# Interleaving two expert layers at their seam, spreading operand splits over two steps, and writing outputs out one block at a time

## Chip, core and metric

The kernel runs on one core of one Trainium2 chip. The metric is the device time of one execution in microseconds (us), as the median of several runs. Five engines work side by side, each through its own queue in the order in which the program emits instructions: TensorE (PE, matrix products, with weight loads shown apart as PEld), VectorE (DVE), ScalarE (ACT), GpSimd (POOL) and SyncE (SP, which here only issues DMAs).

## The reference, cut to what matters

```python
x = rmsnorm_attention(q, k, v, g_norm)            # linear attention, (2304, 512)
h = x @ w_in; x = (h * sigmoid(h)) @ w_out        # first experts: 512 -> 2048 -> 512
p = domain_probs / (domain_probs.sum(-1, keepdims=True) + 1e-9)
out = zeros(2304, 512)
for e in range(4):                                # second experts: 512 -> 1024 -> 512 each
    h = maximum(x @ w1[e], 0)
    out += p[:, e:e+1] * (h @ w2[e])
```

Everything is float32. Each operand is split into a high part and a rest, and a product is the sum of three PE products (high by high, high by rest, rest by high).

## The kernel before

The first part is one hand-written order (`PROGRAM`, and then the loop at L750) of attention and the first experts. The 2048 hidden features are 16 chunks, taken as 4 groups of 4, and the 2304 tokens are five tiles. A unit is one chunk of one tile: `mm1` (12 matmuls into a bank of the PSUM pool `ps_h`, evacuated by ACT and DVE in `ev1` and `ev2`), and two units later (`LAG`) `mm2` (12 matmuls into the four banks of `ps_a`). After the fourth chunk of a tile, `flush` adds the four banks to the SBUF array `acc` on DVE, and the next tile's `mm2` must wait for the banks to be free. `divide` (L709) normalizes the probabilities on DVE, turns them with one PE transpose and sends them to DRAM; it is emitted between an `mm1` and an `mm2`.

The second part is the class `Second`. It has 24 steps: `NP` = 3 token blocks t of 768 tokens, by `E2` = 8 half experts q; n = 8t + q. A step does a 2 by 2 block product in seven products instead of eight (a Strassen-Winograd form): `first(n, k)`, k = 0 to 6, 12 matmuls each, which accumulate into two PSUM tiles x and z of the pool `ps1`. Its weight operands are the sums `sum1` (s1 to s4) split by `op1`, its feature operands the sums `sumx` (t1 to t4) split by `opx`. A split is two instructions: ACT copies the high part (L139), and DVE or POOL subtracts it (L140). Then `keep` (ACT) and `add` (DVE) take the sums out of PSUM, `hid` (ACT, then DVE) makes the hidden blocks, `second(n, b, d)` is 12 matmuls each for four blocks b and two halves d into `ps2` (two tiles of two banks), `weigh` multiplies by the probabilities on DVE, and for q > 0 POOL adds the result to `acc` (L261).

`events` gives each of these a time in slots; a slot is one group of 12 matmuls, and a step is 15 slots. All events are sorted by slot and emitted, so the slots are the order in every queue. `first(n, k)` stands at slot 1 + 2k of step n and the eight `second` of step n at the even places of step n + 1, so the two alternate on PE. Weight operands of step n are made in step n - 1 (`before` is its first slot). For a new token block (q = 0) `opx(t, k)` stands at `before + 2k + 2.5`, so all seven feature operands and four sums are made within step n - 1. The events of step 0 with a slot below zero (`early`) are dealt out over the last eight units of the first experts. After a block's last step `leave` turns the output with PE transposes: two groups of 128 tokens share one tile of `ps2`, each with 4 transposes (L269), an ACT copy (L271) and a DMA issued by ACT (L272).

Of the kernel before, what the change touches and what calls it, by code (L numbers as in the profile page):

```python
# [8 lines left out]
F32 = mybir.dt.float32  # L9
# [4 lines left out]
AF = mybir.ActivationFunctionType  # L14
# [66 lines left out]
class Second:  # L81
# [14 lines left out]
    SLOTS = 15  # L96

    BLOCKS = ((0, 1), (0, 0), (1, 1), (1, 0))

    def __init__(self, tc, w, acc, p_dram, ident, out):  # L100
        self.tc, self.nc = tc, tc.nc
# [9 lines left out]
    def open_right(self):  # L111
# [4 lines left out]
        self.s_p = self.open(st, "s", 3, side="right")  # L116
        self.raw1_p = self.open(st, "raw1", 5, side="right")

    def open_left(self):
        st = ExitStack()  # L120
        self.stacks.append(st)
        self.w2_p = self.open(st, "w2", 5)
        self.raw2_p = self.open(st, "raw2", 4)
        self.h_p = self.open(st, "hid", 6)
        self.f_p = self.open(st, "f", 4)
        self.m_p = self.open(st, "m", 2)
        self.pb_p = self.open(st, "pb", 2)
        self.o_p = self.open(st, "o2", 2)
        self.ps1 = self.open(st, "ps1", 2, space=PSUM)
        self.ps2 = self.open(st, "ps2", 2, space=PSUM)  # L130

    def close(self):
# [63 lines left out]
        self.nc.vector.tensor_tensor(f, b[a], b[c], op=ALU.subtract)  # L196
        self.t[t, name] = f

    def opx(self, t, k):
        name = self.B[k]  # L200
        src = self.t[t, name] if name[0] == "t" else self.sums(t, int(name[1]) - 1, int(name[2]) - 1)
        x = self.x_p.tile([128, 2, 2, HN], F32R, tag=f"x{k}", name="x2")
        self.split(x, src)
        self.x[t, k] = x


# [24 lines left out]
    def hid(self, n, i, j, name):  # L231
# [4 lines left out]
        self.nc.vector.scalar_tensor_tensor(h[:, 1], src, 0.0, h[:, 0].bitcast(F32), op0=ALU.max, op1=ALU.subtract)  # L236
        self.h[n, i, j] = h

    def second(self, n, b, d):
        i, j = self.BLOCKS[b]  # L240
        if d == 0:
            self.ps[n, b] = self.ps2.tile([128, 2, 512], F32, tag="ps2", name="ps_o")
        o = self.ps[n, b][:, d, :HN]
# [9 lines left out]
    def weigh(self, n, b):  # L253
        t, q = divmod(n, E2)
        i, j = self.BLOCKS[b]
        p = self.pb[t, q // 2][:, j * HN : j * HN + HN].unsqueeze(1).to_broadcast([128, 2, HN])
        a = self.sums(t, i, j)
        m = a if q == 0 else self.m_p.tile([128, 2, HN], F32, tag="m", name="m")
        self.nc.vector.tensor_tensor(m, self.ps[n, b][:, :, :HN], p, op=ALU.mult)  # L259
        if q:  # L260
            self.nc.gpsimd.tensor_tensor(a, a, m, op=ALU.add)  # L261

    def leave(self, t, b):

        p = self.ps2.tile([128, 2, 512], F32, tag="ps2", name="ps_t")
        for k in range(2):
            c = (b + k) * 128
            for d in range(KC):
                self.nc.tensor.transpose(p[:, k, d * 128 : d * 128 + 128], self.acc[:, t, d, c : c + 128], self.ident)  # L269
            o = self.o_p.tile([128, DM], F32, tag="o2", name="o2")  # L270
            self.nc.scalar.activation(o, p[:, k, :], AF.Copy)  # L271
            self.nc.scalar.dma_start(out=self.out[t * PW + c : t * PW + c + 128, :], in_=o)  # L272


    def events(self):

        ev = []

        def put(slot, f, *a):
            ev.append((slot, len(ev), f, a))  # L280

        pool = self.nc.gpsimd
        for n in range(self.steps):
            t, q = divmod(n, E2)
# [48 lines left out]
            if q % 2 == 0:  # L333
                put(after - 8, self.load_p, t, q // 2)
            for b in range(4):
                for d in range(2):
                    put(after + 4 * b + 2 * d, self.second, n, b, d)
                put(after + 4 * b + 3.2, self.weigh, n, b)
                put(after + 4 * b + 3.21, self.ps.pop, (n, b))
            for i in range(2):  # L340
                for j in range(2):
                    put(after + (10.1, 14.1)[1 - j], self.h.pop, (n, i, j))
                    put(after + (6.1, 14.1)[i], self.w2.pop, (n, i, j))
            if q % 2 == 1:
                put(after + 15.3, self.pb.pop, (t, q // 2))
            if q == E2 - 1:
                for b in range(0, PW // 128, 2):
# [7 lines left out]
    def run(self):  # L355
        for s, _, f, a in self.events():
            if s >= 0:
                f(*a)


# [1 line left out]
def attention_moe_kernel(ctx: ExitStack, tc: tile.TileContext, kv, qt, g2, probs, wd, w, out):  # L362
    nc = tc.nc


    left, right, psum = ExitStack(), ExitStack(), ExitStack()
# [11 lines left out]
    ring_p = on(left, "ring", RING)  # L378
    h_p = on(left, "h", 3)
    tmp_p = on(left, "tmp", 6)  # L380
    ps_h = on(psum, "ps_h", 4, space=PSUM)
    ps_a = on(psum, "ps_a", 1, space=PSUM)

    ident = const.tile([128, 128], F32, name="ident")
# [302 lines left out]
    with tc.manual_schedule():  # L687
# [21 lines left out]
        def divide():  # L709
# [2 lines left out]
            nc.vector.reciprocal(prs, prs)  # L712
            nb = NT // 128
            nc.vector.tensor_tensor(prn, pr.rearrange("p b e -> p e b"), prs.rearrange("p b o -> p o b").to_broadcast([128, 4, nb]), op=ALU.mult)
            p = ps_h.tile([4 * nb, 128], F32, tag="p", name="p_p")
            nc.tensor.transpose(p, prn.rearrange("p e b -> p (e b)"), ident)
            t = tmp_p.tile([4 * nb, 128], F32, tag="tmp", name="p_t")
# [45 lines left out]
        moe.run()  # L763
        moe.close()


# [32 lines left out]
```

## Time and profile before

| | us |
|---|---|
| median of 3 runs (1280.91 to 1282.31) | 1281.31 |
| the profiled execution | 1280.92 |
| its span, first to last instruction | 1278.8 |
| PE busy in the span | 1225.7 (96%) |
| DVE busy | 743.5 (58%) |
| ACT busy | 497.2 (39%) |
| POOL busy | 490.2 (38%) |
| mean granted TensorE clock | 0.984 of full speed |

The span is cut into stretches below by the times at which PE's groups start. Attention ends at about 165 us, the first experts at 484.8 us, and the 24 steps of the second experts run to 1264 us; what remains is the end of the outputs. In a stretch where PE is the limit, PE's busy time is the stretch itself and its granted clock is 1.00; stretches with a smaller busy time or a lower clock are where time can be won.

### The profile page before, as it was taken

Reading aid. Unit: us, or ns where it says so; the run is one execution under the profiler, and the core shown is the slowest. Engines: PE = TensorE matmul, PEld = TensorE weight load, DVE = VectorE, ACT = ScalarE, POOL = GpSimd, SP = SyncE. Lnnn points to the kernel's source line nnn. Section 1 sums busy time; section 2 is a strip of 40 time slices with the busy share of each in tenths; the row PEclk is TensorE's granted clock in tenths of the full one; section 3 lists DMA queues with packets and bytes.
Section 4 is the critical chain, followed back from the end, with each engine's and each line's share of the span. In section 5 each row is a group of like instructions: output and inputs, shape, how many; then the busy total and the mean of one; then the engine's idle time right before and its main releaser. Section 6 shows DMA issues by size and latency. Waiting matters only on the chain.

```text
span 1278.8 us, 17258 instructions
## 1 busy us (share of the span) xinstructions
PE 1225.7 (96%) x6705; PEld 1149.1 (90%) x6705; DVE 743.5 (58%) x978; ACT 497.2 (39%) x811; POOL 490.2 (38%) x338
## 2 busy tenths in 40 slices
PE   6889999999999988999999899999998999999997
PEld 6778798887888878999999899999998999999996
DVE  4985546554654475565566865555558655665531
ACT  4555443333332244333334434333334443333321
POOL 2563423302300002255555452455554424555543
PEclk9999999998999999999999999999999999999998
DMA  9523111002200013222222133222221223222201
GB/s 329 187 70 108 33 51 51 16 1 100 74 1 1 1 39 107 77 69 79 67 78 67 50 96 100 78 67 82 72 84 47 85 79 85 73 85 68 62 9 49
DMA packets 72981, 91.90 MB, mean 72 GB/s; under 512 B 8956, under 2 KB 62788, under 8 KB 72900
## 3 DMA queue, kind: packets, MB, share of 16 engines
q1 hardware_dynamic: 70020, 86.05, 21.9%
q10 hardware_dynamic: 2880, 4.76, 1.0%
q8 instruction: 52, 0.85, 0.3%
q14 instruction: 29, 0.24, 0.1%
HBM read 86.02 MB, written 4.76 MB: 71 GB/s over the span
## 4 chain that ended last, share of the span: by engine, by line
PE 79%; DVE 5%; ACT 2%; issue 1%; POOLq 0%; POOL 0%; ACTq 0%; DVEq 0%
PE ps_o L250 29%; PE ps_x L217 14%; PE a L656 12%; PE p_h L618 11%; PE ps_z L217 11%; DVE s L176 1%; PE ps_t L269 1%; DVE x L140 1%; DVE t L196 1%; DVE f L229 1%; DVE w L140 1%; ACT o L271 1%; ACT w L139 0%; DVE hid L236 0%; ACT hid L235 0%
## 5 line engine op out<-in xcount | busy, mean ns | idle before, releaser
L250 PE MATMUL ps_o<-hid,w 128*128 128x384 f32 x2304 | 432.4, 337 | 9.4 <-ACT hid L235 7.4
L250 PEld LDWEIGHTS ps_o<-hid,w 128*128 128x128 f32 x2304 | 406.2, 189 | 11.4 <-ACT hid L235 8.3
L140 POOL TENSOR_TENSOR w<-raw,w 128x512 fp32r<-128x512 f32 x144 | 204.0, 1435 | 291.0 <-ACT w L139 169.8
L261 POOL TENSOR_TENSOR acc<-acc,m 128x768 f32<-128x768 f32 x84 | 162.9, 1940 | 254.0 <-DVE m L259 253.9
L217 PE MATMUL ps_x<-x,w 128*128 128x384 f32 x1152 | 217.4, 336 | 1.4 <-DVE f L229 1.4
L217 PEld LDWEIGHTS ps_x<-x,w 128*128 128x128 f32 x1152 | 202.4, 189 | 1.9 <-DVE f L229 1.8
L217 PE MATMUL ps_z<-x,w 128*128 128x384 f32 x864 | 161.8, 335 | 0.0
L217 PEld LDWEIGHTS ps_z<-x,w 128*128 128x128 f32 x864 | 151.0, 188 | 0.2 <-ACT f L224 0.2
L140 DVE TENSOR_TENSOR w<-s,w 128x512 fp32r<-128x512 f32 x96 | 95.1, 992 | 85.0 <-ACT w L139 85.0
L139 ACT ACTIVATE w<-raw 128x512 fp32r<-128x512 f32 x168 | 100.4, 624 | 63.8 <-issue 62.5
L656 PE MATMUL a<-h_hi,w_hi 128*128 128x512 f32 (+1 forms) x320 | 119.9, 375 | 3.5 <-DVE acc L668 3.5
L618 PE MATMUL p_h<-x_hi,w_hi 128*128 128x512 f32 (+1 forms) x320 | 120.3, 376 | 1.0 <-ACT o L554 1.0
L656 PE MATMUL a<-h_lo,w_hi 128*128 128x512 f32 (+1 forms) x320 | 119.3, 373 | 1.1 <-DVE h_lo L642 1.1
L618 PE MATMUL p_h<-x_lo,w_hi 128*128 128x512 f32 (+1 forms) x320 | 119.6, 374 | 0.4 <-DVE x_lo L604 0.4
L618 PE MATMUL p_h<-x_hi,w_lo 128*128 128x512 f32 (+1 forms) x320 | 119.7, 374 | 0.0
L656 PE MATMUL a<-h_hi,w_lo 128*128 128x512 f32 (+1 forms) x320 | 118.9, 372 | 0.0
L633 DVE TENSOR_TENSOR sg<-p_h,sg 128x512 f32<-128x512 f32 (+1 forms) x80 | 50.8, 637 | 102.5 <-ACT sg L632 102.2
L478 POOL TENSOR_TENSOR cv_a<-wd_raw,cv_a 128x512 f32<-128x512 f32 x28 | 37.5, 1340 | 188.8 <-DVE cv_a L476 79.1
L139 ACT ACTIVATE w<-s 128x512 fp32r<-128x512 f32 x96 | 60.2, 628 | 113.8 <-DVE s L176 111.3
L632 ACT ACTIVATE sg<-p_h 128x512 f32<-128x512 f32 (+1 forms) x80 | 44.4, 556 | 150.3 <-PE p_h L618 145.4
L224 ACT ACTIVATE f<-ps_x 128x768 f32<-128x768 f32 x48 | 39.1, 814 | 156.7 <-PE ps_x L217 156.7
L259 DVE TENSOR_TENSOR m<-ps_o,pb 128x768 f32<-128x768 f32 x84 | 80.3, 956 | 29.8 <-PE ps_o L250 27.8
(112 smaller groups left out, 1414.6 us busy)
## 6 DMA issues: line engine op xcount, KB each, us to landing
raw<-in_w SPq DMA_DIRECT2D x384, 128.0 KB, 2.4
wd_raw<-in_wd SPq DMA_DIRECT2D x28, 512.0 KB, 3.8
pb<-p_dram SPq DMA_DIRECT2D x12, 384.0 KB, 4.2
out<-o ACTq DMA_DIRECT2D x18, 256.0 KB, 2.0
kv_first_lo<-in_kv SPq DMA_DIRECT2D x6, 512.0 KB, 9.7
q_raw<-in_qt SPq DMA_DIRECT2D x6, 512.0 KB, 8.1
kv_first_hi<-in_kv SPq DMA_DIRECT2D x5, 512.0 KB, 11.1
acc<-in_wd SPq DMA_DIRECT2D x4, 512.0 KB, 10.9
```

The source lines that it names most:

```text
L139: self.nc.scalar.activation(t[:, 0], f, AF.Copy)
L140: (eng or self.nc.vector).tensor_tensor(t[:, 1], f, t[:, 0].bitcast(F32), op=ALU.subtract)
L217: self.nc.tensor.matmul(p[:, f, :HN], w[:, a, cols], x[:, b, kp, :], start=self.FRESH[k] and kp == m == 0, stop=kp == 1 and m == 2, skip_g ...
L224: self.nc.scalar.activation(t, self.ps[n, c][:, :, :HN], AF.Copy)
L250: self.nc.tensor.matmul(o, w[:, u, cols], h[:, v, kp, :], start=m == 0, stop=m == 11)
L259: self.nc.vector.tensor_tensor(m, self.ps[n, b][:, :, :HN], p, op=ALU.mult)
L261: self.nc.gpsimd.tensor_tensor(a, a, m, op=ALU.add)
L478: nc.gpsimd.tensor_tensor(a, l, a, op=ALU.mult)
L618: nc.tensor.matmul(p[:, :n], wt[:, 0, cols], xt[:, kc, :], start=k == 0, stop=k == 3 * KC - 1)
L632: nc.scalar.activation(sg[:, :n], p[:, :n], AF.Sigmoid)
L633: nc.vector.tensor_tensor(sg[:, :n], p[:, :n], sg[:, :n], op=ALU.mult)
L656: nc.tensor.matmul(o, a, m, start=first and k == 0, stop=last and k == 2)
```

## The change

Five things change.

1. At the seam of the two parts: the PSUM pool of `mm1` is closed before the last two `mm2`, `ps1` is opened in its place, and `first(0, 0)` and `first(0, 1)` are emitted ahead of the last `mm2` but one and the last `mm2`.
2. Feature operands: for t > 0 `opx(t, k)` stands at `before + 3.4k + 4`, so it runs from slot 4 of step n - 1 to slot 9.4 of step n. For t = 0 the subtraction of k = 1, 3, 5 goes to POOL, and for step 0 all seven weight operands' subtractions do (before: two).
3. `leave` takes one group of 128 tokens for a PSUM tile, two calls after each of the first three blocks of the step after next.
4. The last step: blocks in another order (`LAST`), the sum to `acc` on DVE, the last block's two halves in PSUM tiles of their own and weighed apart, and `leave_last`, which turns pieces of the output as soon as they are final (6, 6, 6, 3 and 3 transposes), with DMAs issued by SP.
5. The transpose of the probabilities (`turn_p`) is emitted four units after `divide`.

```diff
+    LAST = ((0, 1), (1, 1), (0, 0), (1, 0))
...
+    def open_first(self):
+        st = ExitStack()
+        self.stacks.append(st)
+        self.ps1 = self.open(st, "ps1", 2, space=PSUM, side="right")
...
-    def opx(self, t, k):
+    def opx(self, t, k, eng=None):
...
-        self.split(x, src)
+        self.split(x, src, eng)
...
+    def end(self, n, b):
+        return n == self.steps - 1 and b == 3
...
-        if d == 0:
-            self.ps[n, b] = self.ps2.tile([128, 2, 512], F32, tag="ps2", name="ps_o")
+        if d == 0 or self.end(n, b):
+            self.ps[n, b, d] = self.ps2.tile([128, 2, 512], F32, tag="ps2", name="ps_o")
...
+            eng = self.nc.vector if n == self.steps - 1 else self.nc.gpsimd
+            eng.tensor_tensor(a, a, m, op=ALU.add)
...
+    def leave(self, t, k):
         p = self.ps2.tile([128, 2, 512], F32, tag="ps2", name="ps_t")
-        for k in range(2):
-            c = (b + k) * 128
-            for d in range(KC):
-                self.nc.tensor.transpose(p[:, k, d * 128 : d * 128 + 128], self.acc[:, t, d, c : c + 128], self.ident)
...
+        c = k * 128
+        for d in range(KC):
+            self.nc.tensor.transpose(p[:, 0, d * 128 : d * 128 + 128], self.acc[:, t, d, c : c + 128], self.ident)
...
+    def leave_last(self, j, ds):
+        t, nk, m = NP - 1, HN // 128, 128 * len(ds)
+        p = self.ps1.tile([128, 2, 512], F32, tag="ps1", name="ps_t").rearrange("p a b -> p (a b)")[:, : nk * m]
+        for k in range(nk):
+            for i, d in enumerate(ds):
+                c, r = j * HN + k * 128, k * m + i * 128
+                self.nc.tensor.transpose(p[:, r : r + 128], self.acc[:, t, d, c : c + 128], self.ident)
+        o = self.f_p.tile([128, 2, HN], F32, tag="f", name="o").rearrange("p a b -> p (a b)")[:, : nk * m]
+        self.nc.scalar.activation(o, p, AF.Copy)
...
+        self.nc.sync.dma_start(out=to, in_=o.rearrange("p (k c) -> p k c", k=nk))
...
-                put(before + 2 * k + 2.3, self.op1, n, k, pool if k in (1, 6) else None)
+                put(before + 2 * k + 2.3, self.op1, n, k, pool if k in (1, 6) or n == 0 else None)
...
-                at = [before + 2 * k + 2.5 for k in range(7)]
+                at = [before + 3.4 * k + 4 for k in range(7)]
...
-                    put(at[k], self.opx, t, k)
+                    put(at[k], self.opx, t, k, pool if t == 0 and k % 2 else None)
...
+                    if last and b == 3:
+                        put(after + 4 * b + 2 * d + 1.2, self.weigh, n, b, d, 1)
...
+            if last:
+                for slot, j, ds in ((6.5, 1, (0, 1)), (10.5, 1, (2, 3)), (12.5, 0, (0, 1)), (15, 0, (2,)), (16, 0, (3,))):
+                    put(after + slot, self.leave_last, j, ds)
...
-                    put(after + 20 + 2 * b, self.leave, t, b)
+                        put(after + self.SLOTS + 4 * (k // 2) + 3.3, self.leave, t, k)
...
+            if s >= 0 and not (f == self.first and a[0] == 0 and a[1] < k):
...
+        put(at[2, 0, 0] + 4, 0, turn_p)
...
-        for u in units[-LAG:]:
+        psum_h.close()
+        moe.open_first()
+        for k, u in enumerate(units[-LAG:]):
+            moe.first(0, k)
             mm2(*u)
```

## Rows read from the trace of the kernel before

**Rows 1.** The page's first part: busy time, share of the span, and instructions by engine.
```profile
PE 1225.7 (96%) x6705; PEld 1149.1 (90%) x6705; DVE 743.5 (58%) x978; ACT 497.2 (39%) x811; POOL 490.2 (38%) x338
```

**Rows 2.** Waits of PE over the span: total us, how many, the longest.
```profile
PE ps_o L250 <- ACT hid L235: 7.4, 3, 2.8
...
PE p_p L716 <- DVE prn L714: 3.8, 1, 3.8
PE a L656 <- DVE acc L668: 3.5, 1, 3.5
```

**Rows 3.** Stretches: length, busy us of each engine, granted clock, DMA share, GB/s.
```profile
286.00:296.63 10.63, 6.87 (x26) 6.01 (x26) 2.24 (x6) 1.50 (x3) 0.00 (x0) 0.68 0.44 152
466.00:473.94 7.94, 4.47 (x14) 3.49 (x14) 6.44 (x11) 2.35 (x6) 0.00 (x0) 0.79 0.12 33
484.82:507.58 22.76, 19.03 (x97) 17.77 (x96) 14.48 (x18) 11.72 (x18) 8.09 (x6) 0.93 0.28 82
659.80:691.10 31.30, 31.30 (x183) 31.30 (x182) 18.74 (x20) 11.86 (x19) 16.17 (x10) 1.00 0.26 81
697.10:728.40 31.30, 27.74 (x159) 27.16 (x157) 26.66 (x27) 15.19 (x22) 12.90 (x7) 1.00 0.14 41
722.14:734.17 12.03, 8.36 (x37) 7.78 (x37) 10.92 (x12) 5.56 (x8) 4.93 (x3) 0.86 0.30 88
983.32:996.25 12.93, 9.49 (x37) 8.78 (x37) 10.92 (x12) 5.55 (x8) 5.84 (x4) 0.74 0.27 81
771.67:775.54 3.87, 3.18 (x22) 2.95 (x20) 2.28 (x3) 1.20 (x2) 0.17 (x1) 1.00 0.28 107
```

**Rows 4.** Chain that ended last: start, us, engine, line and matmuls of a group.
```profile
452.52 2.73 PE p_h L618 x12
...
518.16 2.08 PE ps_o L250 x12
```

**Rows 5.** Timeline, end of the first experts: start, us, engine, instruction, idle before, releaser.
```profile
468.76 2.48 DVE L668 TENSOR_TENSOR acc<-a,acc 128x512 f32<-128x512 f32 x4
```

**Rows 6.** Timeline of an undisturbed step (start 661.7 us): DVE, POOL, PE.
```profile
673.13 0.68 DVE L176 TENSOR_TENSOR s<-raw,raw 128x512 f32<-128x512 f32 x1
...
679.41 4.71 POOL L140 TENSOR_TENSOR w<-raw,w 128x512 fp32r<-128x512 f32 x3
...
681.19 1.77 DVE L176 TENSOR_TENSOR s<-raw,raw 128x512 f32<-128x512 f32 x1
682.88 0.94 DVE L229 TENSOR_TENSOR f<-ps_x,f 128x768 f32<-128x768 f32 x1
...
689.35 0.95 DVE L236 SCALAR_TENSOR_TENSOR hid<-f,hid 128x768 fp32r<-128x768 f32 x1
...
690.90 4.33 PE L250 MATMUL ps_o<-hid,w 128*128 128x384 f32 x24
```

**Rows 7.** Timeline at the seam: the last flush, the next DVE instruction, the first second product.
```profile
482.98 2.74 DVE L668 TENSOR_TENSOR acc<-a,acc 128x512 f32<-128x512 f32 x4 [3.41 <-PE a L656]
488.49 0.69 DVE L140 TENSOR_TENSOR w<-raw,w 128x512 fp32r<-128x512 f32 x1 [2.78 <-ACT w L139]
...
503.39 0.56 PE L250 MATMUL ps_o<-hid,w 128*128 128x384 f32 x1 [1.84 <-ACT hid L235]
```

**Rows 8.** Timeline of the first pair of output groups of the first token block.
```profile
771.67 0.60 PE L269 MATMUL ps_t<-ident,acc 128*128 128x128 f32 x4
...
772.95 0.66 PE L269 MATMUL ps_t<-ident,acc 128*128 128x128 f32 x4 [0.69 <-ACT o L271]
```

**Rows 9.** Timeline of the end, from the last block's weighing to the last DMA issue.
```profile
1264.43 0.96 DVE L259 TENSOR_TENSOR m<-ps_o,pb 128x768 f32<-128x768 f32 x1 [3.21 <-PE ps_o L250]
1265.47 1.80 POOL L261 TENSOR_TENSOR acc<-acc,m 128x768 f32<-128x768 f32 x1 [2.34 <-DVE m L259]
...
1267.33 0.44 PE L269 MATMUL ps_t<-ident,acc 128*128 128x128 f32 x2 [2.78 <-POOL acc L261]
...
1275.97 0.34 ACTq L272 DMA_DIRECT2D out<-o  x1
```

More of the change, by code (lines that the diff above doesn't have):

```diff
@@ L128, in open_left @@
         self.o_p = self.open(st, "o2", 2)
-        self.ps1 = self.open(st, "ps1", 2, space=PSUM)
         self.ps2 = self.open(st, "ps2", 2, space=PSUM)
@@ L237, in hid, with blocks @@
         self.h[n, i, j] = h
+    def blocks(self, n):
+        return self.LAST if n == self.steps - 1 else self.BLOCKS
+    def end(self, n, b):
+        return n == self.steps - 1 and b == 3
     def second(self, n, b, d):
-        i, j = self.BLOCKS[b]
-        if d == 0:
-            self.ps[n, b] = self.ps2.tile([128, 2, 512], F32, tag="ps2", name="ps_o")
-        o = self.ps[n, b][:, d, :HN]
+        i, j = self.blocks(n)[b]
+        if d == 0 or self.end(n, b):
+            self.ps[n, b, d] = self.ps2.tile([128, 2, 512], F32, tag="ps2", name="ps_o")
+        o = self.ps[n, b, d if self.end(n, b) else 0][:, d, :HN]
         m = 0
@@ L251, in second, with weigh @@
                     m += 1
-    def weigh(self, n, b):
+    def weigh(self, n, b, d=0, c=2):
         t, q = divmod(n, E2)
[L255 to L259, printed above, removed]
+        i, j = self.blocks(n)[b]
+        p = self.pb[t, q // 2][:, j * HN : j * HN + HN].unsqueeze(1).to_broadcast([128, c, HN])
+        a = self.sums(t, i, j)[:, d : d + c]
+        m = a if q == 0 else self.m_p.tile([128, 2, HN], F32, tag="m", name="m")[:, :c]
+        self.nc.vector.tensor_tensor(m, self.ps.pop((n, b, d))[:, d : d + c, :HN], p, op=ALU.mult)
@@ L260, in weigh @@
         if q:
-            self.nc.gpsimd.tensor_tensor(a, a, m, op=ALU.add)
-    def leave(self, t, b):
+            eng = self.nc.vector if n == self.steps - 1 else self.nc.gpsimd
+            eng.tensor_tensor(a, a, m, op=ALU.add)
+    def leave(self, t, k):
         p = self.ps2.tile([128, 2, 512], F32, tag="ps2", name="ps_t")
-        for k in range(2):
-            c = (b + k) * 128
-            for d in range(KC):
-                self.nc.tensor.transpose(p[:, k, d * 128 : d * 128 + 128], self.acc[:, t, d, c : c + 128], self.ident)
-            o = self.o_p.tile([128, DM], F32, tag="o2", name="o2")
-            self.nc.scalar.activation(o, p[:, k, :], AF.Copy)
-            self.nc.scalar.dma_start(out=self.out[t * PW + c : t * PW + c + 128, :], in_=o)
+        c = k * 128
+        for d in range(KC):
+            self.nc.tensor.transpose(p[:, 0, d * 128 : d * 128 + 128], self.acc[:, t, d, c : c + 128], self.ident)
+        o = self.o_p.tile([128, DM], F32, tag="o2", name="o2")
+        self.nc.scalar.activation(o, p[:, 0, :], AF.Copy)
+        self.nc.scalar.dma_start(out=self.out[t * PW + c : t * PW + c + 128, :], in_=o)
@@ new lines, in leave_last @@
+    def leave_last(self, j, ds):
[7 more added lines that the diff above has]
+        self.nc.scalar.activation(o, p, AF.Copy)
+        r = t * PW + j * HN
+        to = self.out[r : r + HN, ds[0] * 128 : ds[0] * 128 + m].rearrange("(k p) c -> p k c", p=128)
+        self.nc.sync.dma_start(out=to, in_=o.rearrange("p (k c) -> p k c", k=nk))
@@ L334, in events @@
                 put(after - 8, self.load_p, t, q // 2)
+            last = n == self.steps - 1
             for b in range(4):
@@ L337, in events @@
                     put(after + 4 * b + 2 * d, self.second, n, b, d)
[L338 to L347, printed above, removed]
-                    put(after + 20 + 2 * b, self.leave, t, b)
+                    if last and b == 3:
+                        put(after + 4 * b + 2 * d + 1.2, self.weigh, n, b, d, 1)
+                if not last or b < 3:
+                    put(after + 4 * b + 3.2, self.weigh, n, b)
+            if last:
+                for slot, j, ds in ((6.5, 1, (0, 1)), (10.5, 1, (2, 3)), (12.5, 0, (0, 1)), (15, 0, (2,)), (16, 0, (3,))):
+                    put(after + slot, self.leave_last, j, ds)
+            else:
+                for i in range(2):
+                    for j in range(2):
+                        put(after + (10.1, 14.1)[1 - j], self.h.pop, (n, i, j))
+                        put(after + (6.1, 14.1)[i], self.w2.pop, (n, i, j))
+                if q % 2 == 1:
+                    put(after + 15.3, self.pb.pop, (t, q // 2))
+                if q == E2 - 1:
+                    for k in range(PW // 128):
+                        put(after + self.SLOTS + 4 * (k // 2) + 3.3, self.leave, t, k)
         return sorted(ev, key=lambda e: e[:2])
@@ L353, in early, with run @@
         return [lambda f=f, a=a: f(*a) for s, _, f, a in self.events() if s < 0 and f != self.load2]
-    def run(self):
+    def run(self, k):
         for s, _, f, a in self.events():
-            if s >= 0:
+            if s >= 0 and not (f == self.first and a[0] == 0 and a[1] < k):
                 f(*a)
@@ L363, in attention_moe_kernel @@
     nc = tc.nc
-    left, right, psum = ExitStack(), ExitStack(), ExitStack()
+    left, right, psum, psum_h = (ExitStack() for _ in range(4))
     const = ctx.enter_context(tc.tile_pool(name="const", bufs=1))
@@ L380, in attention_moe_kernel @@
     tmp_p = on(left, "tmp", 6)
-    ps_h = on(psum, "ps_h", 4, space=PSUM)
+    ps_h = on(psum_h, "ps_h", 4, space=PSUM, side="right")
     ps_a = on(psum, "ps_a", 1, space=PSUM)
@@ L714, in divide, with turn_p @@
             nc.vector.tensor_tensor(prn, pr.rearrange("p b e -> p e b"), prs.rearrange("p b o -> p o b").to_broadcast([128, 4, nb]), op=ALU.mult)
+        def turn_p():
+            nb = NT // 128
             p = ps_h.tile([4 * nb, 128], F32, tag="p", name="p_p")
@@ L762, in attention_moe_kernel @@
         moe.open_left()
-        moe.run()
+        moe.run(LAG)
         moe.close()
```

## Prediction

> **What bounds the kernel now.** The page's first part comes first: PE is busy 96% of the span [rows 1], so time is won only where PE pauses, where it runs at a lower clock, or in the end that has no products. The list of PE's waits names who ends the pauses, and that they are few and long: 3.8 us at the probabilities, 3.5 us for a `flush`, 7.4 us in three waits for `hid` [rows 2]. The table of stretches then shows what each place costs, clock included [rows 3]. The scale is the group of 12 matmuls: 2.72 us at 512 columns and 2.08 us at 384 when undisturbed [rows 4]. An undisturbed step has PE busy for all of 31.30 us at clock 1.00, with DVE busy 18.74 us. The step in which a new token block's operands are made has DVE busy 26.66 us of 31.30 [rows 3]; there the in-order DVE queue makes `hid` late.
>
> Losses, as length less groups at full rate [rows 3, 4]. Probabilities: 10.63 less 12 matmuls of 256 columns (half of 2.72, about 1.4), 12 of 512 (2.72) and a transpose (0.1): 6.4 us, of which 3.76 is idle (10.63 - 6.87) and the rest is the clock of 0.68 behind it. Flush: 7.94 - 2.72 = 5.2 us. Seam: 22.76 us for eight groups (16.7): 6.1 us. The two block changes: three groups (6.25) each in 12.03 and 12.93: 5.8 and 6.7, together 12.5 us. Outputs of blocks 0 and 1: a pair adds 3.87 - 2.08 = 1.8 us, six pairs. End: from 1264.0 (last group's end) to 1278.8, 14.8 us.
>
> **The change part by part.** *Probabilities (change 5).* The wait goes: four units later, some 20 us, DVE has long finished. What stays is one transpose, 0.1 us, in the stream, and the DMA to DRAM on SP moves behind some weight loads, long before the step that needs it. Gain 6.3 us. If something else were late there, the idle 3.76 would return; the other units of that loop show no such pause, so I allow 5 to 6.4.
>
> *Earlier splits to POOL (change 2, t = 0).* The flush starts at 468.76 [rows 5], and PE had wanted its bank at 466.0. I follow the queues: DVE and ACT hand each other every piece (a sum 0.7 to 0.95 us on DVE, its copy 0.65 to 0.85 on ACT, its rest on DVE). Moving the rests of k = 1, 3, 5 and of the weights to POOL takes 3 x 0.95 + 3 x 0.69, about 5 us, from DVE ahead of the flush. But `sum1` and `sumx` stay on DVE, ACT still copies every operand before the next `ev1` in its queue, and `flush` still stands behind `ev2` of the last unit. Laid out in that order the flush starts near 467.9 instead of 468.76: 0.8 us. The moved rests take POOL about 1.57 us each beside DVE (three in 4.71), and a DVE sum of two SBUF arrays that overlaps them takes 1.77 instead of 0.68; an `add` out of PSUM, 0.94, does not suffer [rows 6]. That could eat the gain: five overlaps cost more than 5 us of relief. I take 0.8, with -2 (two of those overlaps fall on the chain) and 5.2 (the whole loss) as ends.
>
> The Trainium skill ("SBUF — State Buffer", section "Who interferes with whom") says that VectorE with two SBUF inputs and a GpSimd instruction that reads SBUF take turns for a whole instruction. The trace agrees (1.77 against 0.68 us, and 0.94 unhurt with a PSUM input [rows 6]). It speaks against moving work to POOL.
>
> *Seam (change 1).* PE has the same groups in the same length; two of the seven firsts now lie before the last `mm2`. So after the last `mm2` only five firsts (10.4 us) stand before `second`. The work that decides is DVE's: in the queue the last flush comes before `add`, `hid` and the sums for step 1. Before, that flush ran under the first two firsts, DVE was idle 2.78 us, and the chain from 488.49 to the first `second` at 503.39 took 14.9 us [rows 7]. Now the flush (0.69 a bank, paced by PE) ends 0.9 us after the last `mm2`, and the same chain follows: 0.9 + 14.9 = 15.8 us after it, where PE has 10.4 us of work. Before, it was 503.39 - 484.82 = 18.6 us after the last `mm2`, with 14.6 us of work. Against the same clock on the wall the new `second` starts 4.17 + 15.8 - 18.6 = 1.4 us later. DVE, idle while the two firsts run early, cannot use the time, because its next instruction is the flush. Banks are no obstacle: the last `mm1` is evacuated by 478.2, before PE reaches `first(0, 0)`. I take -1.5. The ends are -4.5 (the pause before k = 6 adds a lower clock for one group and a half) and +3 (DVE's chain shortens by half of its waits for ACT).
>
> *Block change (change 2, t > 0).* Seven operands and four sums, some 11 us of DVE, spread over 20 slots instead of 12. In the undisturbed step the last `hid` ends at 690.30 and `second` needs it at 692.98 (the second group of the row at 690.90): 2.7 us of slack [rows 6]. Into the crowded end of step n - 1 now fall two sums, one copy's wait and one rest (0.95 + 0.95 + 0.9 + 0.95 = 3.75 us, ahead of s4 and the last `add`), so PE pauses for 0.6 to 1.6 us. In step n the last sum and rest (2.8 us, 2.4 of it where DVE was idle, more if POOL's three weight rests overlap) come just before s3, for another 0 to 1.5 us. I take 2.0 us left per change, against 5.8 and 6.7: gain 8.5 us. The ends are 5 (both pauses long, with a lower clock) and 12.5 (no pause). `x` is ready in time for its product: the operand k = 6 at slot 9.4 of the step, its product at 13.
>
> *Outputs (change 3).* The pair's second four transposes waited 0.69 us for ACT's copy, because both used one tile [rows 8]. With two tiles all eight run through (0.86 us, from 4 in 0.43), but the next `second` takes the first of these tiles, whose copy ends 1.28 us after the start (772.95 - 771.67). So 1.4 instead of 1.8 us, six times: 2.2 us. If the pool handed out the tile copied last, it would be 2.3 us, a loss of 3; if no wait stayed, a gain of 5.
>
> *End (change 4).* Removed are POOL's add (1.80) and the chain of transposes and copies that starts at 1267.33 and issues its last DMA at 1275.97, 2.83 us before the end [rows 9]. Added are three pieces of 6 transposes among the last products, 0.64 us each, so the products end at 1264.0 + 1.9 = 1265.9. Their blocks are summed in time: weighing 0.96 and a sum on DVE of about 1.1 against one group plus a piece, 2.7 us. Then: 0.41 to DVE's start (1264.43 - 1264.02), half a block weighed (0.55) and summed (0.55), 0.06, three transposes (0.5), the copy of 384 columns (0.5), and 2.83 from the DMA issue, plus hand-overs: 5.5 us. End near 1271.5, gain 7.3. DMAs in pieces of 512 B could land later, by up to the 2 us that a DMA of whole rows takes: 5.5 to 8.5.
>
> **The sum.** 6.3 + 0.8 - 1.5 + 8.5 + 2.2 + 7.3 = 23.6 us. The profiled execution is 1280.92 us (span 1278.8, 2.1 outside, unchanged), so it gives 1257.3; the median before is 0.4 higher, so 1257.7 us.
>
> **Rivals.** *POOL and DVE collide.* Every POOL rest that meets a DVE sum delays it by about 1.1 us [rows 6], and ten more POOL instructions stand before the seam. Then flush gives -2, the seam -3.5, the block change 5 and outputs 1.5: 6.3 - 2 - 3.5 + 5 + 1.5 + 7.3 = 14.6, so 1266.7 us. The rule of the Trainium skill cited above ("SBUF — State Buffer") would have it go this way. For it: the 1.77; against it: most of DVE's work at those places reads PSUM or waits for ACT anyway. *DVE is freed altogether.* Flush 4.5, seam +1, block change 12, outputs 3, end 8: with 6.3, 34.8, so 1246.5 us. For it: DVE is idle 12.6 us of an undisturbed step; against it: the idle time lies early in the step. *The small output pieces do not do what they are for.* If the last DMAs land as late as now, the end gains 2 instead of 7.3: 1263.0 us. *Slower than before: the lower clock stays.* Behind each long pause the clock was 0.68 to 0.86 of full over the stretch [rows 3]. If the new pauses at the seam followed each other so that a whole step ran at the lower of the two levels (1.2 instead of 2.4 GHz), that step's 31.3 us would double, and 23.6 of gain would become a loss of 8: 1289 us. It decides from about 24 us of full-rate work done at the lower level; before, none of these stretches lost more than 3 us to the clock.
>
> **How the numbers follow.** Forecast 0.50, collision 0.20, freed 0.20, small pieces 0.06, lower clock 0.01; the other 0.03 lies between them. The range 1247 to 1267 us takes in the forecast and its open ends, the pieces, over half of the collision's case and half of the freed one: about 0.8. A measurement of this kernel tells some 0.2%, 2.6 us, from no change: faster 0.97, within it 0.015, slower 0.015.
>
> **What would show it.** No PE wait for `prn`, and `p_p` in the stream. A PE pause for `acc` before the last tile's first `mm2`, about 2.6 us instead of 3.5. At the seam, DVE idle until the last flush, a PE pause before `first(0, 6)` of about 3 us and one before the first `second`. At each block change, pauses of 1 us or less and clock 1.00. Pairs of outputs with PE waiting 0.4 us once, at `second`. The last DMA issue about 2.6 us after the last product. I am wrong if the seam is faster than before, if the flush is in time, or if pauses at the block change are as long as before.

## The result and the profile after

The changed kernel takes 1260.37 us (median of 4 runs, 1259.4 to 1261.1) against 1281.81 us before (1280.9 to 1285.2): a ratio of 0.9827, 95% interval 0.9808 to 0.9847. The forecast was 1257.7 us, in a range of 1247 to 1267. The profiled execution took 1259.40 us with a span of 1257.6, so 21.2 us less span than before.

The page's first part of the changed kernel, to set against [rows 1]: PE has the same 6705 instructions and 10 us less busy time, since it meets the lower clock less; DVE and ACT are as busy as before.

```profile
PE 1215.6 (97%) x6705; PEld 1138.6 (91%) x6705; DVE 746.8 (59%) x976; ACT 496.1 (39%) x810; POOL 499.5 (40%) x342
```

PE's longest waits in the changed kernel, and the one that bears on the outputs (total us, how many, the longest), against [rows 2]. The 3.8 us for the probabilities is gone. The wait of the last `mm2` tile for the flush is still there, 3.1 us. The long waits for `hid` have become more and shorter ones; the first line is of the kernel before, and with the one in [rows 2] it made 9.4 us there, where 6.8 are left.

```profile
PE ps_o L250 <- DVE hid L236: 2.0, 3, 0.9
...
PE ps_o L262 <- DVE hid L241: 4.2, 5, 0.9
PE a L691 <- DVE acc L703: 3.1, 1, 3.1
PE ps_o L262 <- ACT hid L240: 2.6, 4, 1.9
...
PE ps_o L262 <- ACT o L284: 1.4, 6, 0.2
```

The same places as stretches (length, busy us of PE, PEld, DVE, ACT, POOL, then the granted clock, DMA share, GB/s), against [rows 3]: 15 us behind the division of the probabilities, the flush, the seam from the end of the last `mm2` to the end of the first second product, the two pauses of the first block change (those of the second are as long, 5.73 and 5.98 us), a pair of outputs, the last nine groups with the three pieces of output among them, and the end from the last product on.

```profile
285.00:300.00 15.00, 15.00 (x78) 12.74 (x77) 8.14 (x19) 5.95 (x10) 2.95 (x2) 1.00 0.00 1
460.06:470.50 10.44, 7.30 (x25) 5.78 (x25) 6.38 (x10) 3.43 (x6) 3.57 (x4) 0.84 0.19 51
482.95:501.61 18.66, 13.91 (x73) 12.37 (x72) 14.24 (x18) 9.64 (x15) 6.01 (x5) 1.00 0.28 78
716.18:721.91 5.73, 4.70 (x25) 4.13 (x25) 5.73 (x6) 3.95 (x6) 3.59 (x3) 1.00 0.58 174
749.00:754.97 5.97, 4.71 (x26) 4.13 (x26) 5.63 (x7) 3.22 (x5) 4.39 (x3) 1.00 0.53 161
761.22:764.70 3.48, 3.23 (x21) 2.99 (x20) 0.96 (x1) 1.91 (x4) 0.00 (x1) 1.00 0.31 109
1231.26:1252.05 20.79, 20.79 (x127) 20.65 (x127) 8.78 (x10) 3.88 (x5) 3.12 (x2) 1.00 0.12 40
1252.05:1257.60 5.55, 1.01 (x7) 0.56 (x5) 1.11 (x2) 0.98 (x2) 0.00 (x0) 0.89 0.42 136
```

With the same scale as in the forecast (2.72 and 2.08 us a group) these give what each place still costs. Each stretch of a block change holds two groups (4.17 us); that of the flush two of 2.72. The last nine groups need 18.75 us, so the three pieces among them take 2.0 (20.79 - 18.75).

| place | lost before | lost after | won | forecast |
|---|---|---|---|---|
| probabilities | 6.4 | 0.1 | 6.3 | 6.3 |
| flush | 5.2 | 10.44 - 5.44 = 5.0 | 0.2 | 0.8 |
| seam | 6.1 | 18.66 - 12.5 = 6.2 | -0.1 | -1.5 |
| two block changes | 12.5 | 2 x (1.56 + 1.80) = 6.7 | 5.8 | 8.5 |
| outputs, six pairs | 10.8 | 6 x (3.48 - 2.08) = 8.4 | 2.4 | 2.2 |
| end, three pieces (2.0) included | 14.8 | 5.55 + 2.0 = 7.6 | 7.2 | 7.3 |
| sum | | | 21.8 | 23.6 |

The sum is 21.8 where the span fell by 21.2: the execution of after was 0.5 us behind before these places begin (the last `mm1` of 512 columns ahead of the probabilities starts at 283.60, before at 283.07).

### The profile page after: what moved, and what is told of

Read it like the earlier page. It is cut to its first block, busy times and chain, and to the rows that moved or that the text cites. A ratio compares the mean times of both kernels' runs of the same rounds, so it can differ in the third digit from the quotient of the medians.

```text
span 1257.6 us, 17273 instructions
## 1 busy us (share of the span) xinstructions
PE 1215.6 (97%) x6705; PEld 1138.6 (91%) x6705; DVE 746.8 (59%) x976; ACT 496.1 (39%) x810; POOL 499.5 (40%) x342
## 4 chain that ended last, share of the span: by engine, by line
PE 78%; DVE 6%; ACT 2%; issue 1%; DVEq 0%; ACTq 0%
PE ps_o L262 30%; PE ps_x L222 14%; PE a L691 11%; PE ps_z L222 11%; PE p_h L653 11%; DVE w L145 1%; DVE s L181 1%; DVE t L201 1%; DVE f L234 1%; DVE hid L241 1%; ACT x L144 0%; ACT w L144 0%; DVE x L145 0%; DVE m L272 0%; DVE sg L668 0%
## 5 line engine op out<-in xcount | busy, mean ns | idle before, releaser
L262 PEld LDWEIGHTS ps_o<-hid,w 128*128 128x128 f32 x2304 | 401.6, 188 | 12.7 <-DVE hid L241 5.5
L145 POOL TENSOR_TENSOR w<-raw,w 128x512 fp32r<-128x512 f32 x145 | 208.1, 1453 | 160.4 <-ACT w L144 143.0
L275 POOL TENSOR_TENSOR acc<-acc,m 128x768 f32<-128x768 f32 x80 | 157.4, 1968 | 244.4 <-DVE m L272 240.1
L272 DVE TENSOR_TENSOR m<-ps_o,pb 128x768 f32<-128x768 f32 (+1 forms) x85 | 80.4, 945 | 27.1 <-PE ps_o L262 25.0
```

Source lines behind the costliest of these rows:

```text
L145: (eng or self.nc.vector).tensor_tensor(t[:, 1], f, t[:, 0].bitcast(F32), op=ALU.subtract)
L272: self.nc.vector.tensor_tensor(m, self.ps.pop((n, b, d))[:, d : d + c, :HN], p, op=ALU.mult)
L275: eng.tensor_tensor(a, a, m, op=ALU.add)
```

## Experiments

All are changes to the changed kernel, so the number to set them against is its 1260.4 us. Where a difference is a few us, the traces are compared stretch by stretch, because the start of the kernel alone varies by up to 5 us from one profiled execution to the next (the `mm1` at 283.60 in the changed kernel starts at 281.49 in the run with the splits back on DVE, and at 286.47 in that with the transpose back). The kernel before, run again beside the experiments, took 1281.8 to 1283.0 us, so a difference of 1 us between them says nothing.

**The seam undone.** Both last `mm2` come ahead of all firsts again; the rest of the change stays.

```diff
-        psum_h.close()
-        moe.open_first()
-        for k, u in enumerate(units[-LAG:]):
-            moe.first(0, k)
+        for u in units[-LAG:]:
             mm2(*u)
+        psum_h.close()
+        moe.open_first()
...
-        moe.run(LAG)
+        moe.run(0)
```

> The changed kernel with change 1 undone: both last mm2 ahead of all firsts. Theory (the seam is paced by DVE's queue, in which the last flush stands ahead of the sums): within 1.5 us of the changed kernel's 1260.4, with the first second product some 1 us earlier after the seam began, and the pauses of PE bunched again, with a lower clock behind them as in the kernel before. Rival (the two firsts among the last mm2 win time for PE): 1263 us or more.

Measured: 1259.8 us (1257.5 to 1261.0), as with the seam. The timeline of PE (start, us, engine, instruction, idle before, releaser) has pauses of 1.46, 1.84 and 0.55 us, 3.85 in all; with the seam there is one more of 0.77 before them, 4.62 in all.

```profile
492.57 2.38 PE L222 MATMUL ps_x<-x,w 128*128 128x384 f32 x12 [1.46 <-DVE f L234]
496.79 0.44 PE L262 MATMUL ps_o<-hid,w 128*128 128x384 f32 x1 [1.84 <-ACT hid L240]
497.78 2.18 PE L262 MATMUL ps_o<-hid,w 128*128 128x384 f32 x11 [0.55 <-DVE hid L241]
```

So the interleaving wins nothing, and costs 0.8 us of idle time that a run cannot tell. Of the expectation, the lower clock behind the pauses did not come: 11 matmuls in 2.18 us, as with the seam.

**The spread undone.** The seven operands go back into one step.

```diff
-                at = [before + 3.4 * k + 4 for k in range(7)]
+                at = [before + 2 * k + 2.5 for k in range(7)]
```

> The changed kernel with the feature operands of token blocks 1 and 2 back in one step (slots before + 2k + 2.5). Theory (DVE's in-order queue, crowded in one step): the two pauses return as one long one per block change with a lower clock, 12.5 us lost in place of about 6.8, so 1266 us (1265 to 1267.5). Rival (the pauses come from POOL and DVE colliding, whose number does not change): 1262 us or less.

Measured: 1268.3 us (1265.4 to 1269.8), above the 1265 to 1267.5 that were expected. By stretches the two changes lose 12.5 us again where 6.7 stood (three groups each in 12.99 and 12.02 us), which is what was expected; the profiled execution also started 2.0 us later and lost 2.7 us more at the seam, where the clock fell (see the last section). In PE's timeline the long pause is back (the second block change has the same, at 986.7), and with it the clock: 11 matmuls in 3.89 us.

```profile
725.83 0.65 PE L262 MATMUL ps_o<-hid,w 128*128 128x384 f32 x1 [2.75 <-ACT hid L240]
727.18 3.89 PE L262 MATMUL ps_o<-hid,w 128*128 128x384 f32 x11 [0.70 <-DVE hid L241]
```

**The transpose of the probabilities back behind the division.**

```diff
-        put(at[2, 0, 0] + 4, 0, turn_p)
+        put(at[2, 0, 0], 0, turn_p)
```

> The changed kernel with the transpose of the probabilities back right behind their division. Theory: PE waits 3.8 us for the division again and 2.6 us go to the clock behind it, 1266.7 us (1266 to 1267.5). Rival (the pause at this place is taken back by shorter pauses later): 1262 us or less.

Measured: 1269.3 us (1266.0 to 1271.8), above the 1266 to 1267.5 that were expected. PE's wait is back to the last digit of [rows 2], and nothing later makes up for it. In the trace this place loses 5.5 us (from 289.27, the end of the group before, to 299.08, less 4.3 us of work). The profiled execution is 12.4 us longer than that of the changed kernel; 2.9 of them stand ahead of this place (286.47 against 283.60), and 2.8 come at the seam, where the clock fell.

```profile
PE p_p L754 <- DVE prn L749: 3.8, 1, 3.8
```

**The earlier splits back on DVE.**

```diff
-                put(before + 2 * k + 2.3, self.op1, n, k, pool if k in (1, 6) or n == 0 else None)
+                put(before + 2 * k + 2.3, self.op1, n, k, pool if k in (1, 6) else None)
...
-                    put(at[k], self.opx, t, k, pool if t == 0 and k % 2 else None)
+                    put(at[k], self.opx, t, k)
```

> The changed kernel with the subtractions for token block 0 and for step 0 back on DVE as before. Theory (the flush before the last tile is late because it stands behind the evacuation of a later unit in DVE's queue, and ACT and DVE hand over to each other): the flush starts at most 1 us later, 1260.5 to 1261.5 us. Rival A (DVE's load decides): 3 to 5 us slower, 1263.5 to 1265.5. Rival B (collisions with POOL decide): 2 us faster, 1258.5.

Measured: 1261.7 us (1260.2 to 1261.9), just above the 1260.5 to 1261.5 that were expected. The wait for the flush is 3.46 us instead of 3.14. That small difference does not rule out the two rivals, since the run undoes both at once and they work against each other. The rows are this run's sum ahead of the flush, its wait, and the same sum in the changed kernel:

```profile
455.42 0.69 DVE L181 TENSOR_TENSOR s<-raw,raw 128x512 f32<-128x512 f32 x1
...
461.56 0.77 PE L691 MATMUL a<-h_hi,w_hi 128*128 128x512 f32 x1 [3.46 <-DVE acc L703]
...
456.31 1.77 DVE L181 TENSOR_TENSOR s<-raw,raw 128x512 f32<-128x512 f32 x1
```

With the rests on POOL, DVE reaches this sum 1.2 us earlier against PE's work (3.75 us before PE runs out of it at 460.06, against 2.52 before 457.94 in this run). But then the sum takes 1.77 us instead of 0.69, beside POOL's two weight rests (454.55 to 457.53), and at the flush 0.3 us of the lead is left. The medians cannot show that: the profiled execution of this run started 2.1 us ahead, and lost 2.8 us at the seam and over 1 us behind the flush to a lower clock.

**The flush ahead of one evacuation.** For one unit, `ev1` and `ev2` are emitted behind the `mm2` with the flush.

```diff
-            mm1(*units[i])
+            late = i == len(units) - 3
+            mm1(*units[i], evac=not late)
...
             mm2(*units[i - LAG])
+            if late:
+                ev1(*units[i])
+                ev2(*units[i])
```

> The changed kernel with the evacuation of the last unit but two emitted behind the mm2 that ends the tile before the last, so that this tile's flush stands ahead of it in DVE's queue. Theory (queue order): no PE wait for acc before the last tile's first mm2, 5.0 us of idle time and clock won, less up to 2.6 us if the evacuation of the last mm1 is then late for first(0, 0): 1255.4 to 1258. Rival (ACT's hand-overs or collisions with POOL hold DVE): the flush gains less than 1 us, 1259.5 to 1260.5.

Measured: 1256.2 us (1252.0 to 1259.3). In this run's list of PE's waits the entry for `acc` is gone, and no wait takes its place; the longest that remain are for the `hid` of seam and block changes:

```profile
PE ps_o L262 <- DVE hid L241: 4.2, 5, 0.9
PE ps_o L262 <- ACT hid L240: 2.5, 3, 1.9
```

DVE has the same work and POOL the same rests as in the changed kernel, and the sum at this place takes 1.77 us here too. So the wait was there because the flush stood behind `ev2` of a unit whose ACT half waited for two sums; how much DVE had to do, and the collision, only set its length.

**The last flush behind the first events of step 0.** DVE does one weight rest and the first `add` while the last `mm2` runs; the flush follows them.

```diff
-            mm2(*u)
-        psum.close()
+            mm2(*u, held)
...
-        moe.run(LAG)
+        moe.run(LAG, 0, 4.2)
+        for a in held:
+            flush(*a)
         psum.close()
+        moe.open_ps2()
+        moe.run(LAG, 4.2)
```

> The changed kernel with the last flush emitted behind the events of slots 0 to 4.2 of step 0 (the first keep, one weight rest and the first add on DVE), so that DVE does these while the last mm2 runs. Theory (the chain behind the last flush in DVE's queue paces the seam): the chain is 2.4 us shorter, the first second product begins about 13.3 instead of 15.7 us after the last mm2, 1258 us (1257.4 to 1258.8). Rival (the products themselves or ACT pace it): 1260 to 1260.8.

Measured: 1259.2 us (1257.8 to 1260.3), between theory and rival. PE's timeline tells more: the pause of 0.77 is gone, that of 1.44 is 0.56, and the first second product starts 13.3 us after the last `mm2` (495.79 - 482.49) instead of 15.65: the chain is shorter by the 2.4 us expected. But the wait ahead of the second product is as long as ever, and this time the clock fell behind it (11 matmuls in 3.74 us), which took 1.6 us back.

```profile
491.57 2.38 PE L226 MATMUL ps_x<-x,w 128*128 128x384 f32 x12 [0.56 <-DVE f L238]
495.79 0.44 PE L266 MATMUL ps_o<-hid,w 128*128 128x384 f32 x1 [1.83 <-ACT hid L244]
496.78 3.74 PE L266 MATMUL ps_o<-hid,w 128*128 128x384 f32 x11 [0.55 <-DVE hid L245]
```

**Work for step 1 out of the seam's chain.** On top of the last run: s3, s4 and the operands k = 4 and 5 of step 1 move behind the last `add` and `hid` of step 0.

```diff
-                    put(before + 2 * k + 1.7, self.sum1, n, "s3" if k == 4 else "s4")
-                put(before + 2 * k + 2.3, self.op1, ...)
+                    put(before + (14.2 + 0.1 * (k - 4) if n == 1 else 2 * k + 1.7), self.sum1, n, "s3" if k == 4 else "s4")
+                put(before + (14.25 + 0.1 * (k - 4) if n == 1 and k in (4, 5) else 2 * k + 2.3), self.op1, ...)
```

> As the run with the last flush behind the first events of step 0, and with the sums s3, s4 and the operands k = 4 and 5 of step 1 at slots 14.2 to 14.35, behind the last add and hid of step 0 (their loads' successors follow at 14.4). Theory (what stays of the seam's pauses is DVE work for step 1 that stands between the adds of step 0): PE waits less than 1 us in all at the seam in place of 4.6, 1255 to 1257 us. Rival (the chain add, ACT, DVE itself is as long as the pause): pauses of 2.5 us or more, 1258 or more.

Measured: 1255.1 us (1254.4 to 1257.2). The pauses at the seam are 0.88 and 0.55 us, 1.4 in all where less than 1 was expected and 4.6 stood before. Most of the seam's pauses was DVE work for the next step standing between the adds of this one; it includes 1.1 us that the first of these sums lost beside POOL (1.79 us at 491.67 in the changed kernel, just ahead of the `add` for k = 6). What is left, 0.88, stands behind step 0's own chain of `add` and ACT.

```profile
493.73 0.44 PE L266 MATMUL ps_o<-hid,w 128*128 128x384 f32 x1 [0.88 <-ACT hid L244]
494.72 2.21 PE L266 MATMUL ps_o<-hid,w 128*128 128x384 f32 x11 [0.55 <-DVE hid L245]
```

**Operands at other slots.** No operand of a new block between slots 8 and 14 of either step.

```diff
-                at = [before + 3.4 * k + 4 for k in range(7)]
+                at = [before + s for s in (2.05, 4.0, 14.15, 15.5, 17.6, 19.0, 21.0)]
...
+                        s = {"t1": 7.3, "t2": 7.35}.get(self.B[k]) if t else None
...
```

> The changed kernel with the operands of blocks 1 and 2 at other slots: the two sums t1 and t2 at 7.3, the operands at 2.05, 4.0, 14.15, 15.5, 17.6, 19.0 and 21.0, so that slots 8 to 14 of both steps hold none. Same work and same engines. Theory (crowding of DVE's queue in those slots makes hid late): the four pauses of 1.6 to 1.8 us vanish or fall under 0.4 us, 1254 to 1256 us. Rival (collisions with POOL, as many as before, or the load of the two steps as a whole): 1259 us or more.

Measured: 1258.3 us (1257.9 to 1263.2), between theory and rival: 2.1 us won where 4.4 to 6.4 were expected. The pause in the step before the change is gone at both changes. The one in the step after it stayed, 0.39 and 0.94 us. Timelines of DVE, POOL and PE in that step:

```profile
738.96 0.95 DVE L272 TENSOR_TENSOR m<-ps_o,pb 128x768 f32<-128x768 f32 x1
740.09 2.30 DVE L145 TENSOR_TENSOR w<-s,w 128x512 fp32r<-128x512 f32 x1 [0.18 <-ACT w L144]
742.32 1.77 DVE L181 TENSOR_TENSOR s<-raw,raw 128x512 f32<-128x512 f32 x1
...
745.86 1.89 DVE L241 SCALAR_TENSOR_TENSOR hid<-f,hid 128x768 fp32r<-128x768 f32 x1
...
739.99 1.85 POOL L275 TENSOR_TENSOR acc<-acc,m 128x768 f32<-128x768 f32 x1 [6.78 <-DVE m L272]
741.79 5.15 POOL L145 TENSOR_TENSOR w<-raw,w 128x512 fp32r<-128x512 f32 x3
...
751.02 0.44 PE L262 MATMUL ps_o<-hid,w 128*128 128x384 f32 x1 [0.39 <-ACT hid L240]
752.40 2.20 PE L262 MATMUL ps_o<-hid,w 128*128 128x384 f32 x11 [0.94 <-DVE hid L241]
```

POOL's three weight rests start 9.2 us ahead of the second product (741.79 to 751.02), where they start 13.6 us ahead in an undisturbed step (679.41 to 692.98 in [rows 6]). They wait for POOL's add, which waits for the weighing on DVE at 738.96, and that stood behind operand k = 6. So the add and then the rests run beside DVE's critical instructions, which take 2.30 instead of 0.69 (beside the add), 1.77 instead of 0.68 and 1.89 instead of 0.95.

**The weighing ahead.** The same, but with k = 4, 5 and 6 each behind an instruction that others wait for.

```diff
-                at = [before + s for s in (2.05, 4.0, 14.15, 15.5, 17.6, 19.0, 21.0)]
+                at = [before + s for s in (2.05, 4.0, 14.15, 15.5, 18.25, 19.6, 22.4)]
...
-                        s = {"t1": 7.3, "t2": 7.35}.get(self.B[k]) if t else None
+                        s = {"t1": 7.3, "t2": 7.35, "t3": 17.5}.get(self.B[k]) if t else None
```

> As the run with other slots for the operands of blocks 1 and 2, but the operands k = 4, 5, 6 at 18.25, 19.6 and 22.4 (k = 6 behind the weighing of the second block, k = 4 behind that of the first) and the sum t3 at 17.5. Theory (in that run the weighing stood behind k = 6 in DVE's queue, so POOL's add and its three weight rests ran 5 us later and collided with four DVE instructions, 1.8 to 2.3 us each): the pause of 1.3 us in the second step goes as well, no pause over 0.4 us at the block changes, 1254 to 1256.5 us. Rival (DVE's load over the second step as a whole): the pause stays, 1257.5 or more.

Measured: 1255.7 us (1254.9 to 1256.1). The first part of the pause, for the high half of `hid`, is gone; 0.54 and 0.56 us for its rest stay, a little over the 0.4 that was allowed:

```profile
752.17 2.18 PE L262 MATMUL ps_o<-hid,w 128*128 128x384 f32 x11 [0.54 <-DVE hid L241]
```

The collisions are fewer but not gone. At this place three DVE instructions still lose 0.67, 1.10 and 1.09 us beside POOL (1.62, 1.79 and 1.77 us long, from 739.76 on), 2.9 us in all, where the three of the run before lost 3.6. The pause shrank by as much, from 1.33 to 0.54 us. How much of it order alone would have won, with POOL idle, no run tells.

**The rests last.** In every second product the eight matmuls with the high half of `hid` come first.

```diff
-        for f in range(2):
-            for kp in range(2):
+        for vs in (((0, 0), (1, 0)), ((0, 1),)):
+            for f, kp in ((0, 0), (0, 1), (1, 0), (1, 1)):
...
-                for u, v in ((0, 0), (0, 1), (1, 0)):
+                for u, v in vs:
```

> The changed kernel with the 12 matmuls of a second product in another order: the eight that use the high part of hid first, the four that use its rest last. Theory (a pause has two parts, one for the high part from ACT and 0.9 us for its rest from DVE, and the second is met at the second matmul): the second part is covered by 1.2 us of matmuls at the two block changes (four times 0.9) and at the seam (0.55), 1256.3 us (1255.5 to 1257.5). Rival (the later end only moves the pause to the next product): 1259.5 us or more.

Measured: 1256.4 us (1254.7 to 1258.2). No product waits for a rest any more; of the pauses at the block changes 0.58 us for the high half stayed, and 0.47 moved to the product before it (1004.14 at the second change):

```profile
1004.14 2.33 PE L222 MATMUL ps_x<-x,w 128*128 128x384 f32 x12 [0.47 <-DVE f L234]
1009.13 2.36 PE L262 MATMUL ps_o<-hid,w 128*128 128x384 f32 x12 [0.58 <-ACT hid L240]
```

**All of these together**: the early flush, the seam's new order, the last slots, the rests last.

> The changed kernel with the early flush, the seam's new order on DVE, the last slots for the operands, and the rests last in the second products. Theory (each pause has its own place in a queue, so the gains add up): about 5 from the flush, 4 from the seam and 6.5 from the block changes, 1245 us (1243 to 1248). Rival (a pause that goes lets the next one come forward): 1251 or more.

Measured: 1242.9 us (1242.6 to 1245.3), a ratio of 0.9694 to the kernel before (0.9671 to 0.9717), and 17.5 us under the changed kernel. That is 0.1 under the range that was expected (1243 to 1248); the four single gains (4.2, 5.3, 4.7 and 4.0 us) make 18.1, so they nearly add up. From 270 us on, PE has three kinds of wait left, 3.3 us in all:

```profile
PE ps_o L266 <- ACT o L288: 1.4, 6, 0.2
PE ps_t L298 <- DVE acc L279: 1.0, 1, 1.0
PE ps_o L266 <- ACT hid L244: 0.9, 1, 0.9
```

## Why the prediction was right, and where it was off

The forecast of 1257.7 us is 2.7 us under the median. The mechanism was right: few long pauses, each with an owner in DVE's queue, and an end without products. Term by term (the row numbers are those of before):

*Probabilities.* Right, 6.3 us; undoing it alone brings the wait back.

*Flush.* Right in kind: 0.8 forecast, 0.2 measured, and the wait is 3.1 us where about 2.6 was expected. The term was the relief of DVE alone. The relief came (1.2 us by the run with the splits back on DVE), but one of the overlaps that I had set into the lower end fell on the chain: the first of the two sums in front of the flush took 1.77 us instead of 0.69. So the rival of collisions was at work here, with one overlap and not two.

*Seam.* The step "the same chain follows: 0.9 + 14.9 = 15.8 us after it" holds: the first second product starts 15.65 us after the last `mm2`. DVE did idle until the flush, 7.68 us. These are its row, PE's rows behind it, and as the last one PE's in the kernel before (504.39):

```profile
481.09 2.75 DVE L703 TENSOR_TENSOR acc<-a,acc 128x512 f32<-128x512 f32 x4 [7.68 <-PE a L691]
...
490.56 2.38 PE L222 MATMUL ps_z<-x,w 128*128 128x384 f32 x12 [0.77 <-ACT f L229]
494.39 2.36 PE L222 MATMUL ps_x<-x,w 128*128 128x384 f32 x12 [1.44 <-DVE f L234]
498.60 0.45 PE L262 MATMUL ps_o<-hid,w 128*128 128x384 f32 x1 [1.86 <-ACT hid L240]
499.59 2.18 PE L262 MATMUL ps_o<-hid,w 128*128 128x384 f32 x11 [0.55 <-DVE hid L241]
...
504.39 3.36 PE L250 MATMUL ps_o<-hid,w 128*128 128x384 f32 x11 [0.43 <-DVE hid L236]
```

That it cost 0.1 and not 1.5 us is the clock: the granted clock of the stretch was 0.93 before [rows 3] and is 1.00 now (11 matmuls in 2.18 us instead of 3.36), although the pauses grew from 3.7 (22.76 - 19.03) to 4.6 us. This is luck of two executions and no gain of change 1: with the seam undone the same 11 matmuls took 2.18 us too, and in other runs with the seam as here up to 3.89. The pause before k = 6 is 1.44 us, not about 3; half of the difference is that k = 5 had already waited 0.77 for a `keep`, which I had not followed in ACT's queue.

*Block change.* This term was the most off: "I take 2.0 us left per change" was 3.4, so the gain was 5.8 and not 8.5 us, near the lower end of 5. The first pause was forecast at 0.6 to 1.6 and cost 1.56; the second at 0 to 1.5 and cost 1.80, more than its upper end. My 2.0 lay in the middle of the two ranges together (0.6 to 3.1). Two things were missed.

First, a pause has two parts, one for the high half of `hid` from ACT and one for its rest from DVE, met one matmul later. At all four places the second part is 0.88 to 0.94 us, however short the first; it fell to 0.54 and 0.56 only where the first was gone altogether (the run with the weighing ahead). Second, DVE's added work meets POOL's: the sum of a feature operand falls among POOL's weight rests, and an operand ahead of a `weigh` sets POOL late, as the two runs with other slots show. These are rows of the second step in the changed kernel:

```profile
738.12 1.80 DVE L145 TENSOR_TENSOR w<-s,w 128x512 fp32r<-128x512 f32 x1 [0.68 <-ACT w L144]
739.84 2.04 DVE L201 TENSOR_TENSOR t<-acc,t 128x768 f32<-128x768 f32 x1
...
743.78 1.78 DVE L181 TENSOR_TENSOR s<-raw,raw 128x512 f32<-128x512 f32 x1
...
739.31 3.73 POOL L145 TENSOR_TENSOR w<-raw,w 128x512 fp32r<-128x512 f32 x2
...
751.57 0.44 PE L262 MATMUL ps_o<-hid,w 128*128 128x384 f32 x1 [0.33 <-ACT hid L240]
752.95 2.18 PE L262 MATMUL ps_o<-hid,w 128*128 128x384 f32 x11 [0.94 <-DVE hid L241]
```

The three DVE instructions lose 1.1 us each; in the undisturbed step one does [rows 6], and one loses 0.56. I had put "more if POOL's three weight rests overlap" beside this term and no number. The Trainium skill ("SBUF — State Buffer", section "Who interferes with whom") has the rule by which a VectorE instruction with two SBUF inputs waits out a GpSimd one that reads SBUF; the rows at 740 us of the run with other slots agree (2.30 instead of 0.69 us). So the rival built on it was at work, at the flush with one overlap and here with more, but not to the size of its sum: 1266.7 us was its time, and 1260.4 was measured. Its count was off as well: eight more POOL instructions stand before the seam (three feature and five weight rests), not ten.

*Outputs.* Right: 1.40 us a pair, with one wait of 0.2 us at `second` (0.4 forecast) in place of the 0.69 of [rows 8].

*End.* Right to 0.1 us. The rows that answer to [rows 9]: half a block weighed and summed in 0.56 us each on DVE, three transposes, a copy of 0.49, and 3.0 us from its end to the end of the span.

```profile
1252.25 0.56 DVE L272 TENSOR_TENSOR m<-ps_o,pb 128x384 f32<-128x384 f32 x1 [1.62 <-PE ps_o L262]
...
1253.55 0.52 PE L294 MATMUL ps_t<-ident,acc 128*128 128x128 f32 x3 [1.01 <-DVE acc L275]
1254.15 0.49 ACT L296 ACTIVATE o<-ps_t 128x384 f32<-128x384 f32 x1 [1.09 <-PE ps_t L294]
```

The small pieces land in time (192 KB in rows of 512 B in 2.1 us by the list of DMAs, 256 KB in whole rows in 2.0 before), so that rival fell. The lower clock, the rival on the slower side, did not last anywhere: the mean clock rose from 0.984 to 0.995. (One reading of that rival was a little off: the second block change had lost 6.7 us, of them 3.4 idle (12.93 - 9.49), so 3.2 and not at most 3 went with the clock.)

The sum is nearer than its terms: the block changes fell 2.7 us short, and 1.4 of that came back at the seam by the clock, which nobody had forecast.

## What to carry to other kernels

Where one engine is busy 96% of the time, look for its few long pauses and ask which in-order queue stood in front: here the transpose of the probabilities stood ahead of products that were ready, and the other long pauses in the products were instructions queued behind work that nobody needed yet. Changing the order alone won 17.5 us on top of the change; moving the earlier splits to POOL won 0.3 us of idle time, because most of the lead that DVE got by it was lost again in a collision. Follow a delayed instruction to those who wait for it: an operand set ahead of a weighing set POOL late, and POOL then slowed the instructions that mattered. When a product is the consumer, let it begin with the operands that are ready first.

## What the runs showed of the hardware that was not expected

Behind the same pauses the clock fell in some executions and not in others. At the seam, after a pause of 1.8 us and one of 0.3 to 0.6 ahead of the second product, its other 11 matmuls took 2.18 us in the changed kernel, in the run with the seam undone and in that with the first other slots; 2.94 in that with the last slots, 3.35 with the early flush, 3.74 with the flush behind the first events, and 3.89 with the splits back on DVE, with the spread undone and with the transpose back. Counted to the next second product, so with the group between them, it is 5.1 us in the first three, 6.7 in the next three and 7.8 to 7.9 in the last three. So a pause of some 2 us has a price between nothing and 2.8 us that a single profile does not show; why it differs stays open.
